# Head 0 of an attention kernel: half of K turned by the DMA engine, query halves shifted on chip, and head 1's K loaded later

## The chip, the cores and the metric

The kernel runs on one core of one Trainium2 chip. The metric is the device time of one execution in microseconds (us), as the median of several executions. The profile shows the work of TensorE (PE in the profile; PEld are its weight loads), VectorE (DVE), ScalarE (ACT), GpSimd (POOL) and SyncE (SP), side by side: in the kernel before PE is busy for 99% of the span, ACT for 60%, DVE for 33%, POOL for 15%. In its trace the DMA transfers are issued from the instruction streams of SP (K, V, x), POOL (W, the query moves) and ACT (the output, at 1751.7 to 1934.2 us), and engines wait for their landing, PE for instance 3.1 us for `xnT` (the list of waits below).

This case is about differences of 0.1 to 0.5%, so the scatter matters, and the document comes back to it.

## The reference, cut to what matters

```python
# B = 1, Sq = Sk = 2048, D = 640, H = 32 heads, Dh = 192, F = 1536; everything bf16
def _A_ref(x, k_cache, v_cache, wq, wo):
    q = (x @ wq) -> (B, H, Sq, Dh)
    scores = jnp.einsum("bhqd,bhkd->bhqk", q, k_cache) * (Dh ** -0.5)
    p = _softmax(scores, axis=-1)
    o = jnp.einsum("bhqk,bhkd->bhqd", p, v_cache)
    return o -> (B, Sq, H * Dh) @ wo

def _B_ref(x, w1, w3, w2):                      # SwiGLU feed-forward
    return (silu(x @ w1) * (x @ w3)) @ w2

x = A_x
xn = _layernorm(x, axis=-1)                     # no scale, no bias
return x + _A_ref(xn, ...) * silu(_B_ref(xn, ...))
```

## The kernel before: the parts that the change touches

The main loop walks over 32 heads, 4 query blocks of 512 rows (`qb`) and 8 steps (`p`), each step two key tiles. In every step PE makes the scores of step n + 2 and the values of step n. Once in every block it also projects the next head's queries for the same block. By the trace a step is 1.317 us of PE, a projection 2.16 us, and a steady block 12.69 us. What is special in head 0 is that everything has to be made ready first, while PE is already running:

- `xn`, the normalized x, is turned into `xnT` (D on the partitions). Blocks 0 and half of 1 are turned by PE, the rest by a transposing DMA.
- `xnS` is a copy of `xnT` with its two partition halves exchanged, made by two DMAs. The projections for head 1 and later need both.
- K is needed as five 128-wide windows of pairs of key rows (`KW`). Head 0's K is loaded plainly and turned by PE; later heads use a transposing DMA.
- `qC` holds shifted halves of the projected queries. Block 1 of head 0 shifts on DVE; the others by DMA from POOL (`move_q`).

`project0(qb)` projects head 0's own block qb; `project(1, qb)` projects head 1's block qb. The two are the landmarks of this document.

```python
    def load_k(h):


        pairs_of = A_k_cache[0, h].rearrange("(j two) d -> j (two d)", two=2)
        KW = kvp.tile([P, 5, HK], BF16, tag="KW", name="KW")
        nc.sync.dma_start_transpose(out=KW[:, 0:3, :], in_=pairs_of)
        nc.sync.dma_start_transpose(out=KW[:, 3:5, :], in_=pairs_of[:, 64:64 + 2 * P])
        loads.setdefault(h, {}).update(KW=KW)

    k0 = {}
    WINDOWS = (0, P, 2 * P, 64, 64 + P)

    def load_k0():
        k0["kn"] = stp.tile([P, NQT, HG * DH], BF16, tag="ostage", name="kn")
        kn = k0["kn"][:].rearrange("p t c -> p (t c)")[:, 0:NKT * DH]
        nc.sync.dma_start(out=kn, in_=A_k_cache[0, 0].rearrange("(p t) d -> p (t d)", p=P))
        k0["v"] = kn.rearrange("p (j c) -> p j c", c=2 * DH)
        loads.setdefault(0, {}).update(KW=kvp.tile([P, 5, HK], BF16, tag="KW", name="KW"))

    FIRST = (0, 1, 2, 4)

    def turn_k0(dst, j0, sel):
        for a in sel:
            w = WINDOWS[FIRST[a]]
            for b in range(NPAIR // 2):
                nc.tensor.transpose(out=dst[:, a, b * P:(b + 1) * P], in_=k0["v"][:, j0 + b, w:w + P],
                                    identity=ident_bf[:])

    def copy_k0(src, j0):
        KW = loads[0]["KW"]
        ks = slice(j0 * P, (j0 + NPAIR // 2) * P)
        nc.scalar.copy(out=KW[:, 0:2, ks], in_=src[:, 0:2, :])
        nc.scalar.copy(out=KW[:, 2:5:2, ks], in_=src[:, 2:4, :])

    def shift_k0(j0):
        KW = loads[0]["KW"]
        ks = slice(j0 * P, (j0 + NPAIR // 2) * P)
        nc.gpsimd.dma_start(out=KW[0:64, 3, ks], in_=KW[64:P, 0, ks])

    def load_v(h):
        vt = vts[h % 2]
        if h == 0:
            nc.sync.dma_start(out=vt[:, :, 0:DH], in_=A_v_cache[0, h].rearrange("(i s) d -> i s d", i=P))
        else:
            for t in range(2):
                nc.sync.dma_start(out=vt[:, :, 0:DH].rearrange("i (p t) d -> i p t d", t=2)[:, :, t, :],
                                  in_=A_v_cache[0, h].rearrange("(p i t) d -> i p t d", i=P, t=2)[:, :, t, :])
        loads.setdefault(h, {}).update(vt=vt)
# ... cut: the statistics and 1/sqrt(var + eps) of x: ln_stats, ln_stats_act, ln_rstd ...
    def ln_norm(g, i, engine):
        mv, _, rstd = lnorm[g]
        if (g, i) not in xns:
            xns[g, i] = xnp.tile([P, D], BF16, tag="xn", name="xn")
        engine.tensor_scalar(out=xns[g, i][:], in0=x_sb[:, 4 * g + i, :], scalar1=mv[:, i, 0:1], scalar2=rstd[:, i, 0:1],
                             op0=ALU.subtract, op1=ALU.mult)

    def ln_turn(g, i2, copy):
        pst = ps_st.tile([P, 2, DC, P], BF16, tag="st2", name="pst")
        for k in range(2):
            xn = xns.pop((g, 2 * i2 + k))
            for c in range(DC):
                nc.tensor.transpose(out=pst[:, k, c, :], in_=xn[:, c * P:(c + 1) * P], identity=ident_bf[:])
        q0 = (4 * g + 2 * i2) * P
        copy(out=xnT[:, :, q0:q0 + 2 * P].rearrange("p c (k q) -> p k c q", k=2), in_=pst[:])

    def ln_turn_dma(g, i):
        q0 = (4 * g + i) * P
        nc.sync.dma_start_transpose(out=xnT[:, :, q0:q0 + P], in_=xns.pop((g, i))[:])

    def swap_halves(g):
        qs = slice(g * 512, (g + 1) * 512)
        nc.sync.dma_start(out=xnS[0:64, :, qs], in_=xnT[64:P, :, qs])
        nc.sync.dma_start(out=xnS[64:P, :, qs], in_=xnT[0:64, :, qs])
# ... cut ...
    def move_q(qAB, qC, half):
        nc.gpsimd.dma_start(out=qC[0:64, half, :], in_=qAB[half][64:P, :])
        if half == 0:
            nc.gpsimd.dma_start(out=qC[64:P, 0, :], in_=qAB[0][0:64, :])
# ... cut ...
    def project0(qb):
        W = loads[0]["W"]
        qAB, qC = q_tiles(0, qb)
        qs = slice(qb * 512, (qb + 1) * 512)
        ps = ps_st.tile([P, 1024], F32, tag="st2", name="ps0")
        for half in range(2):
            for c in range(DC):
                nc.tensor.matmul(ps[:, half * 512:(half + 1) * 512], lhsT=W[:, half * DC + c, :], rhs=xnT[:, c, qs],
                                 start=(c == 0), stop=(c == DC - 1))
        cast_pair(qAB, ps)
        if qb == 1:
            nc.vector.tensor_copy(out=qC[64:P, 0, :], in_=qAB[0][0:64, :])
            nc.vector.tensor_copy(out=qC[0:64, 0, :], in_=qAB[0][64:P, :])
            nc.vector.tensor_copy(out=qC[0:64, 1, :], in_=qAB[1][64:P, :])
        else:
            move_q(qAB, qC, 0)
            move_q(qAB, qC, 1)
# ... cut ...
    def two_products(W, qs):

        ps = ps_st.tile([P, 1024], F32, tag="st2", name="ps")
        for j in range(2 * DC):
            for r in range(2):
                rows = slice(r * 64, (r + 1) * 64)
                xs = xnT if j % 2 == r else xnS
                nc.tensor.matmul(ps[:, r * 512:(r + 1) * 512], lhsT=W[rows, j, :], rhs=xs[rows, j // 2, qs],
                                 start=(j == 0), stop=(j == 2 * DC - 1))
        return ps

    def cast_pair(qAB, ps):
        a = nc.vector.tensor_copy(out=qAB[0][:], in_=ps[:, 0:512])
        b = nc.scalar.copy(out=qAB[1][:], in_=ps[:, 512:1024])

        tc.declare_no_dep(b.ins, a.ins, reason="two banks, two destinations")

    def project(h, qb):
        qAB, qC = q_tiles(h, qb)
        cast_pair(qAB, two_products(loads[h]["W"], slice(qb * 512, (qb + 1) * 512)))
        move_q(qAB, qC, 0)
        move_q(qAB, qC, 1)
# ... cut ...
        ov = [obanks[r][:].rearrange("p (j w) -> p j w", j=4)[:, :, 0:DH + 1] for r in range(2)]
        osum = osp.tile([P, 4, DH + 1], F32, tag="osum", name="osum")
        nc.vector.tensor_copy(out=osum[:], in_=ov[0])
        nc.vector.tensor_tensor(out=osum[:], in0=osum[:], in1=ov[1], op=ALU.add)
        osums[0] = osum
```

The start, the work hung onto the steps of head 0, and the loop:

```python
    def head_start():

        load_x(0, 0, 2)
        load_x(0, 2, 4)
        load_k0()
        load_w0()
        load_x(1)
        load_v(0)
        load_w(1)
        turn_over(40)
        ln_stats(0, 0)
        ln_stats(0, 1)
        ln_stats_act(0, 3)
        ln_stats(0, 2)
        ln_rstd(0, 3)
        ln_norm(0, 0, nc.vector)
        ln_norm(0, 1, nc.vector)
        ln_norm(0, 2, nc.vector)
        ln_norm(0, 3, nc.vector)
        pk0 = ps_o.tile([P, 4, 512], BF16, tag="ob0", name="pk0")
        turn_k0(pk0, 0, range(4))
        copy_k0(pk0, 0)
        shift_k0(0)
        turn_over(6)
        ln_turn(0, 0, nc.vector.tensor_copy)
        turn_over(6)
        turn_k0(pk1, NPAIR // 2, range(2))
        ln_turn(0, 1, nc.vector.tensor_copy)
        turn_k0(pk1, NPAIR // 2, range(2, 4))
        swap_halves(0)
        copy_k0(pk1, NPAIR // 2)
        shift_k0(NPAIR // 2)
        for g in range(2, NQB):
            load_x(g)
        project_first()
        scores(0)
        shift_first()
        scores(1)
        ln_stats(1, 0)
        ln_stats(1, 1)
        ln_stats(1, 2)
        ln_norm(1, 0, nc.vector)
        ln_norm(1, 1, nc.vector)
        ln_turn_dma(1, 0)
        ln_turn_dma(1, 1)
        ln_stats(1, 3)
# ... cut ...
    def first_head(qb, p):

        if qb == 0 and p == 1:
            ln_norm(1, 2, nc.vector)
            ln_norm(1, 3, nc.vector)
        if qb == 0 and p == 4:
            ln_turn(1, 1, nc.vector.tensor_copy)
            swap_halves(1)
        g = qb + 2
        if g < NQB:
            i = p - 2
            if 0 <= i < 4:
                ln_stats(g, i)
            for i2 in range(2):
                if p == (4, 6)[i2]:
                    for i in (2 * i2, 2 * i2 + 1):
                        ln_norm(g, i, nc.vector)
                        ln_turn_dma(g, i)
            if p == 6:
                swap_halves(g)
        if qb == 1 and p == 0:
            load_k(1)
            load_v(1)

    for n, (h, qb, p) in enumerate(stream):
        if p == 0 and n > 0:
            if h + 1 < H:
                project(h + 1, qb)
            else:
                ffn_open(qb)
        if h == 0 and qb == 0 and p == 3:
            project(1, 0)
        if h == 0 and qb + 1 < NQB and p == (5 if qb == 0 else 2):
            project0(qb + 1)
        scores(n + 2)
        values(n)
        if p == 0 and n > 0:
            finish_block(n - 1)
        if p == (5 if h == 0 else 2) and h < 2 * NPIG:
            swiglu(h, qb)
        if p == 4 and h + 1 == H:
            ffn_close(qb)
        if h == 0:
            first_head(qb, p)
```

`turn_over(k)` is a row of k dummy matmuls that keep PE going.

## Time and profile before

Before the change the kernel took 1953.1 us in the median of three executions, from 1952.4 to 1957.39. The execution that was profiled has a span of 1951.6 us.

| what | before | where it shows |
|---|---|---|
| PE busy | 1930.7 us, 99% of the span | the page, part 1 |
| PE's share of the chain that ended last | 97% | the page, part 4 |
| period of a block from head 1 on | 12.69 us | the PE timeline |
| first score matmul | 16.30 us | the PE timeline |
| `project(1, 3)` starts | 74.38 us | the PE timeline |

The first two lines are these, from the page of the kernel before (busy time, share and number of instructions of each engine; then the share of the chain that each engine holds):

```profile
...
PE 1930.7 (99%) x27281; PEld 1320.4 (68%) x27289; DVE 653.5 (33%) x991; ACT 1180.7 (60%) x1276; POOL 285.6 (15%) x510
...
PE 97%; DMA 1%; issue 0%; DVE 0%; POOL 0%; SPq 0%; DVEq 0%; POOLq 0%
...
```

PE is the bound. Only PE waits can be won, and after 74 us there are none. So the whole question lies in the first 75 us. I call the start of `project(1, 3)`, the first landmark after which the pattern repeats, **the mark**.

The waits of PE between 13 and 76 us, in the kernel before (what PE waited for, us in total, number of waits, the longest):

```profile
...
PE ps L407 <- DMA xnT<-xn: 3.1, 1, 3.1
PE st L489 <- DMA qC<-qA: 3.0, 1, 3.0
PE st L488 <- DMA KW<-KW: 1.0, 1, 1.0
PE ps L407 <- DVE xnT L354: 0.9, 1, 0.9
PE obank L517 <- DVE osum L527: 0.8, 1, 0.8
...
```

The view counts a wait from the modelled end of the last matmul, so it shows somewhat less than a stop costs in the distance between two landmarks. I use both.

The two largest waits come from the SP queue and the traffic behind it. The timeline of SP in the kernel before (start, duration, operation, destination and source):

```profile
...
38.23 2.52 SPq L358 DMA_TRANSPOSE xnT<-xn  x2
...
43.45 5.59 SPq L252 DMA_TRANSPOSE KW<-in_A_k_cache_dram  x1
49.08 4.28 SPq L253 DMA_TRANSPOSE KW<-in_A_k_cache_dram  x1
53.41 1.21 SPq L292 DMA_DIRECT2D vt<-in_A_v_cache_dram  x2
54.66 6.16 SPq L358 DMA_TRANSPOSE xnT<-xn  x4
...
```

An issue of a transposing load holds the SP queue for 4.28 and 5.59 us here. Head 1's K (L252, L253) and V stand in the queue ahead of the four transposes of xn (54.66), and the small `qC` moves of block 2 (64 KB each), issued at 45.98 to 46.99 us while K is moving, take 5.8 to 7.0 us to land, against a median of 1.9 us in this trace.

### The profile page before, as it was taken

To read this page: it belongs to the slowest core of one execution; us is meant where nothing else is said; L and a number is where in the kernel's file an instruction comes from. 1 tells how busy PE (TensorE), PEld (TensorE's weight loads), DVE (VectorE), ACT (ScalarE), POOL (GpSimd) and SP (SyncE) were. 2 spreads that over 40 slices of the span, in tenths; PEclk is the share of its full clock that TensorE was granted. 3 is DMA by queue.
4 is the path that set the end of the run, shared out by engine and by line. 5 is a ranking of instruction groups with operands and counts; after the bars stand their busy time and mean duration, and the time that the engine had idled before them with its cause. 6 is when DMAs were issued, how large, how long until landed. Compare 5 with 4: busy or idle time off the path is not lost.

```text
span 1951.6 us, 59687 instructions
## 1 busy us (share of the span) xinstructions
PE 1930.7 (99%) x27281; PEld 1320.4 (68%) x27289; DVE 653.5 (33%) x991; ACT 1180.7 (60%) x1276; POOL 285.6 (15%) x510
## 2 busy tenths in 40 slices
...
GB/s 179 135 66 92 52 98 63 90 66 97 63 97 68 100 68 100 68 157 67 100 68 100 68 99 65 100 68 79 87 61 90 59 81 2 239 81 138 154 152 60
DMA packets 394659, 179.50 MB, mean 92 GB/s; under 512 B 341632, under 2 KB 382848, under 8 KB 394400
## 3 DMA queue, kind: packets, MB, share of 16 engines
...
## 4 chain that ended last, share of the span: by engine, by line
PE 97%; DMA 1%; issue 0%; DVE 0%; POOL 0%; SPq 0%; DVEq 0%; POOLq 0%
PE obank L517 35%; PE st L488 33%; PE ps L425 14%; PE ps_s L111 11%; PE ps_f L723 3%; PE ps_gu L697 1%; PE st L489 1%; DMA x_all<-in_A_x_dram 0%; DMA kn<-in_A_k_cache_dram 0%; DMA qC<-qA 0%; PE ps L407 0%; DMA xnT<-xn 0%; DVE qA L430 0%; PE pk L272 0%; POOL rstd L325 0%
## 5 line engine op out<-in xcount | busy, mean ns | idle before, releaser
L491 ACT ACTIVATE pT<-st 128x1024 bf16<-128x1024 f32 x1024 | 1047.3, 1023 | 256.6 <-PE st L489 241.1
L517 PEld LDWEIGHTS <-pT 64*128 64x128 bf16 x16384 | 715.0, 94 | 242.5 <-issue 1.3
L517 PE MATMUL obank<-vt,pT 64*128 64x193 bf16 x16384 | 853.1, 243 | 0.8 <-DVE osum L527 0.8
L488 PE MATMUL st<-qC,KW 64*128 64x512 bf16 x2046 | 605.6, 376 | 1.2 <-DMA KW<-KW 1.0
L526 DVE COPY osum<-obank 128x772 f32<-128x772 f32 x128 | 123.2, 962 | 790.1 <-PE obank L517 790.1
L489 PE MATMUL st<-qC,KW 64*128 64x512 bf16 x1022 | 384.3, 376 | 3.0 <-DMA qC<-qA 3.0
L489 PE MATMUL st<-qB,KW 64*128 64x512 bf16 x1024 | 385.0, 376 | 0.0
L488 PE MATMUL st<-qA,KW 64*128 64x512 bf16 x1022 | 384.3, 376 | 0.3 <-ACT pT L491 0.3
L489 PE MATMUL st<-qA,KW 64*128 64x512 bf16 x1022 | 384.3, 376 | 0.0
L488 PEld LDWEIGHTS <-KW 64*128 64x128 bf16 x3068 | 277.9, 94 | 156.7 <-issue 5.5
L425 PE MATMUL ps<-xnT,W 64*128 64x512 bf16 x1280 | 297.3, 376 | 0.0
L425 PE MATMUL ps<-xnS,W 64*128 64x512 bf16 x1280 | 295.8, 376 | 0.0
L489 PEld LDWEIGHTS <-KW 64*128 64x128 bf16 x3068 | 278.1, 94 | 1.6 <-issue 0.5
L375 POOL DMA_DIRECT2D qC<-qA x126 | 66.2, 526 | 1293.6 <-DVE rl_all L533 1280.7
L431 ACT CAST qB<-ps 128x512 bf16<-128x512 f32 x131 | 76.8, 586 | 233.7 <-PE ps L425 223.3
L111 PE MATMUL ps_s<-wo_sb,oT 128*128 128x384 bf16 (+3 forms) x1535 | 208.8, 299 | 0.1
L425 PEld LDWEIGHTS <-W 64*128 64x128 bf16 x2560 | 123.4, 94 | 121.1 <-issue 0.2
L111 PEld LDWEIGHTS <-oT 128*128 128x128 bf16 x1536 | 148.3, 98 | 60.5
L527 DVE TENSOR_TENSOR osum<-osum,obank 128x772 f32<-128x772 f32 x128 | 122.7, 959 | 13.4
L534 DVE TENSOR_TENSOR ostage<-osum,rl_all 128x768 bf16<-128x768 f32 x128 | 122.6, 958 | 4.4
L466 DVE SCALAR_TENSOR_TENSOR hT<-pt,qB 64x512 bf16<-64x512 bf16 x64 | 43.8, 684 | 203.6 <-ACT pt L465 203.6
L430 DVE CAST qA<-ps 128x512 bf16<-128x512 f32 x131 | 90.6, 692 | 27.7 <-PE ps L407 9.8
...
## 6 DMA issues: line engine op xcount, KB each, us to landing
...
qC<-qA POOLq DMA_DIRECT2D x252, 64.0 KB, 1.9
...
```

The costliest lines, as they stand in the source:

```text
L111: nc.tensor.matmul(ps[:, 0:w], lhsT=oT[:, k, :], rhs=wo_sb[:, k, c0:c1], start=(k == 0), stop=(k == OC - 1))
L375: nc.gpsimd.dma_start(out=qC[0:64, half, :], in_=qAB[half][64:P, :])
L425: nc.tensor.matmul(ps[:, r * 512:(r + 1) * 512], lhsT=W[rows, j, :], rhs=xs[rows, j // 2, qs], start=(j == 0), stop=(j == 2 * DC - 1))
L430: a = nc.vector.tensor_copy(out=qAB[0][:], in_=ps[:, 0:512])
L431: b = nc.scalar.copy(out=qAB[1][:], in_=ps[:, 512:1024])
L488: nc.tensor.matmul(st2[:, 0:512], lhsT=ka, rhs=qa, start=r == 0 and nr == 3, stop=r == nr - 1)
L489: nc.tensor.matmul(st2[:, 512:1024], lhsT=kb, rhs=qb2, start=r == 0 and nr == 3, stop=r == nr - 1)
L491: nc.scalar.activation(out=pT2[:], in_=st2[:], func=ACT.Exp, scale=att_scale)
L517: nc.tensor.matmul(obanks[r][:, j * 256:j * 256 + DH + 1], lhsT=pT2[r * 64:(r + 1) * 64, t * 512 + j * P:t * 512 + (j + 1) * P], rhs=vt[r ...
L526: nc.vector.tensor_copy(out=osum[:], in_=ov[0])
L527: nc.vector.tensor_tensor(out=osum[:], in0=osum[:], in1=ov[1], op=ALU.add)
L534: nc.vector.tensor_tensor(out=ostage[:, qb * 4:qb * 4 + 4, hg * DH:(hg + 1) * DH], in0=osum[:, :, 0:DH], in1=rl.unsqueeze(2).to_broadcast( ...
```

## The change

The intent is to remove five losses of the start at once. Only the first half of head 0's K is turned by PE; the second half comes by a transposing load. K's shift and all query shifts of head 0 are made by DVE. The second turn of block 1 comes a step earlier, the second pair of norms of a later block comes behind the copies of the value banks (`osum`), and head 1's K and V are issued behind the last norms. The variance arithmetic is also regrouped (cut below; what it is worth was not measured).

```diff
@@ -254,43 +254,48 @@
         loads.setdefault(h, {}).update(KW=KW)
 
     k0 = {}
-    WINDOWS = (0, P, 2 * P, 64, 64 + P)
+    FIRST = (0, P, 2 * P, 64 + P)
+    HP = NPAIR // 2
 
     def load_k0():
-        k0["kn"] = stp.tile([P, NQT, HG * DH], BF16, tag="ostage", name="kn")
-        kn = k0["kn"][:].rearrange("p t c -> p (t c)")[:, 0:NKT * DH]
-        nc.sync.dma_start(out=kn, in_=A_k_cache[0, 0].rearrange("(p t) d -> p (t d)", p=P))
+        kn = stp.tile([P, NQT, HG * DH], BF16, tag="ostage", name="kn")
+        kn = kn[:].rearrange("p t c -> p (t c)")[:, 0:NPAIR * DH]
+        nc.sync.dma_start(out=kn, in_=A_k_cache[0, 0, 0:HK, :].rearrange("(p t) d -> p (t d)", p=P))
         k0["v"] = kn.rearrange("p (j c) -> p j c", c=2 * DH)
         loads.setdefault(0, {}).update(KW=kvp.tile([P, 5, HK], BF16, tag="KW", name="KW"))
 
-    FIRST = (0, 1, 2, 4)
-
-    def turn_k0(dst, j0, sel):
+    def load_k0_rest():
+        pairs_of = A_k_cache[0, 0, HK:SK, :].rearrange("(j two) d -> j (two d)", two=2)
+        KW = loads[0]["KW"]
+        nc.sync.dma_start_transpose(out=KW[:, 0:3, HP * P:HK], in_=pairs_of)
+        nc.sync.dma_start_transpose(out=KW[:, 3:5, HP * P:HK], in_=pairs_of[:, 64:64 + 2 * P])
+
+    def turn_k0(dst, sel):
         for a in sel:
-            w = WINDOWS[FIRST[a]]
-            for b in range(NPAIR // 2):
-                nc.tensor.transpose(out=dst[:, a, b * P:(b + 1) * P], in_=k0["v"][:, j0 + b, w:w + P],
+            for b in range(HP):
+                nc.tensor.transpose(out=dst[:, a, b * P:(b + 1) * P], in_=k0["v"][:, b, FIRST[a]:FIRST[a] + P],
                                     identity=ident_bf[:])
 
-    def copy_k0(src, j0):
+    def copy_k0(src):
         KW = loads[0]["KW"]
-        ks = slice(j0 * P, (j0 + NPAIR // 2) * P)
-        nc.scalar.copy(out=KW[:, 0:2, ks], in_=src[:, 0:2, :])
-        nc.scalar.copy(out=KW[:, 2:5:2, ks], in_=src[:, 2:4, :])
-
-    def shift_k0(j0):
+        nc.scalar.copy(out=KW[:, 0:2, 0:HP * P], in_=src[:, 0:2, :])
+        nc.scalar.copy(out=KW[:, 2:5:2, 0:HP * P], in_=src[:, 2:4, :])
+
+    def shift_k0():
         KW = loads[0]["KW"]
-        ks = slice(j0 * P, (j0 + NPAIR // 2) * P)
-        nc.gpsimd.dma_start(out=KW[0:64, 3, ks], in_=KW[64:P, 0, ks])
+        nc.vector.tensor_copy(out=KW[0:64, 3, 0:HP * P], in_=KW[64:P, 0, 0:HP * P])
 
     def load_v(h):
+
+
         vt = vts[h % 2]
+        p0 = 0
         if h == 0:
-            nc.sync.dma_start(out=vt[:, :, 0:DH], in_=A_v_cache[0, h].rearrange("(i s) d -> i s d", i=P))
-        else:
-            for t in range(2):
-                nc.sync.dma_start(out=vt[:, :, 0:DH].rearrange("i (p t) d -> i p t d", t=2)[:, :, t, :],
-                                  in_=A_v_cache[0, h].rearrange("(p i t) d -> i p t d", i=P, t=2)[:, :, t, :])
+            nc.sync.dma_start(out=vt[:, 0:NPAIR, 0:DH], in_=A_v_cache[0, h, 0:HK, :].rearrange("(i s) d -> i s d", i=P))
+            p0 = HP
+        for t in range(2):
+            nc.sync.dma_start(out=vt[:, 2 * p0:NKT, 0:DH].rearrange("i (p t) d -> i p t d", t=2)[:, :, t, :],
+                              in_=A_v_cache[0, h, 2 * p0 * P:SK, :].rearrange("(p i t) d -> i p t d", i=P, t=2)[:, :, t, :])
         loads.setdefault(h, {}).update(vt=vt)
 
     mhalf = const.tile([P, 4], F32, name="mhalf")
 # ... cut: the epsilon is added for two rows at once; ScalarE's statistics leave POOL out ...
@@ -388,8 +395,9 @@
                 for c in range(DC):
                     nc.tensor.matmul(ps[:, half * 512:half * 512 + 256], lhsT=W[:, half * DC + c, :], rhs=xnT[:, c, hs],
                                      start=(c == 0), stop=(c == DC - 1))
-            for half in range(2):
-                nc.vector.tensor_copy(out=qAB[half][:, hs], in_=ps[:, half * 512:half * 512 + 256])
+            i0 = nc.vector.tensor_copy(out=qAB[0][:, hs], in_=ps[:, 0:256])
+            i1 = nc.scalar.copy(out=qAB[1][:, hs], in_=ps[:, 512:768])
+            tc.declare_no_dep(i1.ins, i0.ins, reason="two banks, two destinations")
         nc.vector.tensor_copy(out=qC[0:64, 1, :], in_=qAB[1][64:P, :])
 
     def shift_first():
@@ -407,13 +415,9 @@
                 nc.tensor.matmul(ps[:, half * 512:(half + 1) * 512], lhsT=W[:, half * DC + c, :], rhs=xnT[:, c, qs],
                                  start=(c == 0), stop=(c == DC - 1))
         cast_pair(qAB, ps)
-        if qb == 1:
-            nc.vector.tensor_copy(out=qC[64:P, 0, :], in_=qAB[0][0:64, :])
-            nc.vector.tensor_copy(out=qC[0:64, 0, :], in_=qAB[0][64:P, :])
-            nc.vector.tensor_copy(out=qC[0:64, 1, :], in_=qAB[1][64:P, :])
-        else:
-            move_q(qAB, qC, 0)
-            move_q(qAB, qC, 1)
+        nc.vector.tensor_copy(out=qC[64:P, 0, :], in_=qAB[0][0:64, :])
+        nc.vector.tensor_copy(out=qC[0:64, 0, :], in_=qAB[0][64:P, :])
+        nc.vector.tensor_copy(out=qC[0:64, 1, :], in_=qAB[1][64:P, :])
 
     def two_products(W, qs):
 
@@ -575,36 +579,37 @@
         load_k0()
         load_w0()
         load_x(1)
+        load_k0_rest()
         load_v(0)
-        load_w(1)
         turn_over(40)
         ln_stats(0, 0)
         ln_stats(0, 1)
         ln_stats_act(0, 3)
         ln_stats(0, 2)
+        mv, ve, _ = lnorm[0]
+        nc.vector.tensor_scalar(out=ve[:, 2, :], in0=mv[:, 2, 1:2], scalar1=eps, scalar2=None, op0=ALU.add)
+        nc.vector.tensor_scalar(out=ve[:, 3, :], in0=lnorm["ss"][:], scalar1=1.0 / D, scalar2=eps,
+                                op0=ALU.mult, op1=ALU.add)
         ln_rstd(0, 3)
-        ln_norm(0, 0, nc.vector)
-        ln_norm(0, 1, nc.vector)
-        ln_norm(0, 2, nc.vector)
-        ln_norm(0, 3, nc.vector)
+        load_w(1)
+        for i in range(4):
+            ln_norm(0, i, nc.vector)
         pk0 = ps_o.tile([P, 4, 512], BF16, tag="ob0", name="pk0")
-        turn_k0(pk0, 0, range(4))
-        copy_k0(pk0, 0)
-        shift_k0(0)
-        turn_over(6)
-        ln_turn(0, 0, nc.vector.tensor_copy)
-        turn_over(6)
-        turn_k0(pk1, NPAIR // 2, range(2))
+        ln_turn(0, 0, nc.scalar.copy)
+        turn_over(4)
+        turn_k0(pk0, range(2))
+        turn_over(4)
         ln_turn(0, 1, nc.vector.tensor_copy)
-        turn_k0(pk1, NPAIR // 2, range(2, 4))
+        turn_k0(pk0, range(2, 4))
+        turn_over(4)
         swap_halves(0)
-        copy_k0(pk1, NPAIR // 2)
-        shift_k0(NPAIR // 2)
+        copy_k0(pk0)
         for g in range(2, NQB):
             load_x(g)
         project_first()
         scores(0)
         shift_first()
+        shift_k0()
         scores(1)
         ln_stats(1, 0)
         ln_stats(1, 1)
@@ -627,7 +632,7 @@
         if qb == 0 and p == 1:
             ln_norm(1, 2, nc.vector)
             ln_norm(1, 3, nc.vector)
-        if qb == 0 and p == 4:
+        if qb == 0 and p == 3:
             ln_turn(1, 1, nc.vector.tensor_copy)
             swap_halves(1)
         g = qb + 2
@@ -636,13 +641,13 @@
             if 0 <= i < 4:
                 ln_stats(g, i)
             for i2 in range(2):
-                if p == (4, 6)[i2]:
+                if p == (4, 7)[i2]:
                     for i in (2 * i2, 2 * i2 + 1):
                         ln_norm(g, i, nc.vector)
                         ln_turn_dma(g, i)
-            if p == 6:
+            if p == 7:
                 swap_halves(g)
-        if qb == 1 and p == 0:
+        if qb == 1 and p == 7:
             load_k(1)
             load_v(1)
 
@@ -654,7 +659,7 @@
                 ffn_open(qb)
         if h == 0 and qb == 0 and p == 3:
             project(1, 0)
-        if h == 0 and qb + 1 < NQB and p == (5 if qb == 0 else 2):
+        if h == 0 and qb + 1 < NQB and p == (5 if qb == 0 else 3):
             project0(qb + 1)
         scores(n + 2)
         values(n)
```

## The prediction

> **What bounds the kernel now.** TensorE: PE is 97% of the chain of waits, and from 74.5 us on the same line (head 1's projection for the last query block) recurs every 12.69 us without a gap. The change only touches the head, about 4% of the span; 2% (39 us) is out of reach. By the timeline, PE work between the first score (16.30 us) and 74.5 us is 26 score groups of 0.65, 24 value groups of 0.67, six projections of 2.16 and one turn of 0.56: 46.4 us in 58.2. About 12 us are lost there (PE timeline, waits):
> 1. 2 us before score group 2, for the K shift by DMA (KW<-KW, issued 12.3/14.9, landed 19.8/21.8).
> 2. 1.4 us at 28.6-30.3, projection waiting for xnT's copy after a late turn.
> 3. 1.1 us at 39.5, value group waiting for osum, behind two norms on DVE.
> 4. 3.1 us at 50.4-53.5, scores waiting for qC<-qA (7.0 us to land among head 1's K transposes; usually 1.9).
> 5. 3.1 us at 61.1-64.2, projection waiting for xnT<-xn, queued behind head 1's K (43.5-53.4) and V.
>
> **What the change does.** It halves the plain K load (768 to 384 KB) and adds a 512-row transposing load. PE loses 16 K transposes (0.06 us each), ACT two 1.0 us copies, but gains one xnT copy (estimate 1.2 us) and two half casts. DVE takes K's shift and the query shifts of blocks 2 and 3: 0.29 us each, in idle DVE time. Turn 1 moves to p=3, the second norms behind the osum copies, K1/V1 behind block 3's norms (about 57 us instead of 43; head 1 needs them at about 73, a whole K plus V took 15 us).
>
> **Costed.** Loss 4: -3.1. Loss 5: -2.6: the norms start about 2.1 us after the block's end, take 0.8, and the second transpose lands about 6.4 after it, where PE asks at 6.1; 0.3-0.6 us of wait stay, in block 1 too. Loss 3: -1.0. Loss 2: -1.2. Start and loss 1: PE alone could gain 4-5 us, but DMA is at 9 tenths nearly throughout 2-25 us, and bytes up to the xnS swap hardly fall (estimate 4.45 MB against 4.32). W0's last piece landed at 12.9, xnS at 23.0 (needed at 23.6), x block 2 at 25.0. If these stay, the first projection ends no earlier than 14.5 (now 15.5) and head 1's first begins no earlier than 22.5: gain about 1 us. [...]
>
> Sum: about 8 us. Predicted **1945.0 us, 1941.0 to 1949.5**. Faster by over 2%: 0.01; within 2%: 0.98; slower: 0.01.
>
> **What would show it.** The projection at 74.5 us starts at 66-67. No qC<-qA wait in head 0's scores; K1's transposes issued after 55 us; waits for xnT<-xn of at most 0.7 us each; first score near 15.0; project(1,0) at 22.5-23.5, after a wait for xnS; the 12.69 us period unchanged.
>
> **What would make it wrong.** A transposing load slow in the crowded start: K's second half, V and xnS come late and 1-3 us go. DMA lighter than I think: the gain is 11-12 us. Norms at p=7 pushing xnT later: 2-3 us return. K1 or V1 too late: head 1 stalls.

What is cut, at the end of "Costed", are two sentences of reasons for W0's slow landing and for the rate of the start that did not come from this case. No term of the sum is cut: losses 4, 5, 3 and 2 with 3.1, 2.6, 1.0 and 1.2 us and the start with about 1 make 8.9, less the 0.3 to 0.6 us of wait that stay in block 1; that is the "about 8". What the trace of before shows: W0's three loads on POOL (160, 80 and 80 KB) took 8.07, 8.70 and 9.38 us from issue to landing beside the loads on SP, and the core moved 334 GB/s from 7 to 10 us and 179 from 10 to 14. Why they were slow it doesn't show; that they would stay so was my estimate. The landing of `xnS` that the forecast gives as 23.0 us is 23.70 in that trace. The 1.2 us for a copy of `xnT` on ACT are an estimate; ACT's copy of K, four fifths as wide, took 1.02 us in before, and in after the copy of `xnT` took 1.23.

## The result, and the profile after

| | before | after |
|---|---|---|
| median of four fast runs (lowest to highest) | 1952.75 us (1948.89 to 1957.39) | 1950.75 us (1949.44 to 1952.48) |
| ratio, after over before | | 0.9989 (0.9965 to 1.0013) |
| span of the profiled run | 1951.6 us | 1947.9 us |
| the mark | 74.38 us | 70.77 us |

A ratio here stands on record with each timed set: it is worked out from the fast runs of both kernels in the same rounds, so it isn't quite the ratio of the medians. The brackets are a 95% interval. The class is "same" at 2%. The change gained about 2 us where 8 were predicted, and 1950.75 lies above the predicted range, 1941.0 to 1949.5.

The lines of the page of the kernel after that answer to those of before:

```profile
...
PE 1930.6 (99%) x27273; PEld 1318.3 (68%) x27273; DVE 653.1 (34%) x996; ACT 1179.5 (61%) x1277; POOL 282.5 (15%) x501
...
PE 97%; DMA 1%; DVE 1%; ACT 0%; issue 0%; POOL 0%; SPq 0%; POOLq 0%; DVEq 0%; ACTq 0%
...
```

PE does the same work in the same time; what changed is waiting. The waits of PE in the same window, in the kernel after:

```profile
...
PE ps L415 <- DMA xnT<-xn: 3.8, 2, 2.6
PE ps L429 <- DMA xnS<-xnT: 2.7, 1, 2.7
...
PE st L488 <- DVE qA L398: 0.6, 1, 0.6
...
```

The waits for `qC`, `osum` and `KW` are gone, as predicted. The wait for `xnT` is not smaller, it is larger: two waits, 3.8 us together, instead of one of 3.1. A wait for `xnS` of 2.7 us is new. 

The SP timeline shows where both come from. First the start, in the kernel before and then in the kernel after:

```profile
...
2.61 0.69 SPq L289 DMA_DIRECT2D vt<-in_A_v_cache_dram  x1
14.04 0.64 SPq L362 DMA_DIRECT2D xnS<-xnT  x1
14.72 0.62 SPq L363 DMA_DIRECT2D xnS<-xnT  x1
...
```

```profile
...
2.62 5.07 SPq L270 DMA_TRANSPOSE KW<-in_A_k_cache_dram  x1
7.74 3.63 SPq L271 DMA_TRANSPOSE KW<-in_A_k_cache_dram  x1
11.41 0.69 SPq L294 DMA_DIRECT2D vt<-in_A_v_cache_dram  x1
12.15 1.47 SPq L297 DMA_DIRECT2D vt<-in_A_v_cache_dram  x2
13.74 2.14 SPq L369 DMA_DIRECT2D xnS<-xnT  x1
15.92 0.62 SPq L370 DMA_DIRECT2D xnS<-xnT  x1
...
```

V's load was issued at 2.61 us before and is issued at 11.41 us after, because the two transposing loads hold the queue for 5.07 and 3.63 us. The swap into `xnS` is issued behind V, and lands at 24.2 us (23.7 before), although everything ahead of it was meant to be lighter. PE arrives at `project(1, 0)` at 21.21 us and stands there until 24.30.

Then blocks 1 and 2, in the kernel after:

```profile
...
38.94 2.52 SPq L365 DMA_TRANSPOSE xnT<-xn  x2
...
50.50 7.51 SPq L365 DMA_TRANSPOSE xnT<-xn  x4
61.81 0.60 SPq L369 DMA_DIRECT2D xnS<-xnT  x1
...
63.12 5.20 SPq L252 DMA_TRANSPOSE KW<-in_A_k_cache_dram  x1
```

Head 1's K (63.12) now stands behind everything, as intended. The transposes of block 1's second half are issued at 38.94 us, and those of block 2 at 55.48 (the last two of the four in the line of 50.50), but the landings are late, as the sums below show.

### Where the time went, stretch by stretch

A block of head 0 is 8 steps and two projections. By the trace's own durations that is 8 x 1.317 + 2 x 2.16 = 14.86 us of PE (an estimate from those). The distance from one `project(1, qb)` to the next, less 14.86, is what the block loses.

| stretch | before | after | gained | predicted |
|---|---|---|---|---|
| start of the span to `project(1, 1)` | 36.49 | 36.17 | 0.3 | about 2.2 (start 1, turn 1.2) |
| block 1: to `project(1, 2)` | 19.46 | 16.54 | 2.9 | 3.5 to 3.8 (4.1 less the rest wait) |
| block 2: to `project(1, 3)` | 18.43 | 18.06 | 0.4 | 2.6 |
| sum, the mark | 74.38 | 70.77 | 3.6 | about 8 |

So two terms failed: the start and block 2. Block 1 is some 0.7 us short, for the same reason as block 2, as will show.

The traces gain 3.6 us and the medians 2.0. The runs of the kernel before explain why the two need not agree. In the largest set (11 runs beside the third group of experiments) its times fall into two clusters, 1949.12 to 1949.73 (5 runs) and 1952.21 to 1953.76 (6 runs). The traced execution of before belongs to the upper cluster, that of after to the quick end of its own runs (1949.65). What puts an execution of before into one cluster or the other I have not traced.

### The profile page after: what moved, and what is told of

It reads as the page before. It is cut to its first block, busy times and chain, and to the rows that moved or that the text cites. A ratio compares the mean times of both kernels' runs of the same rounds, so it can differ in the third digit from the quotient of the medians.

```text
span 1947.9 us, 59661 instructions
## 1 busy us (share of the span) xinstructions
PE 1930.6 (99%) x27273; PEld 1318.3 (68%) x27273; DVE 653.1 (34%) x996; ACT 1179.5 (61%) x1277; POOL 282.5 (15%) x501
## 3 DMA queue, kind: packets, MB, share of 16 engines
q8 instruction: 215, 3.52, 0.8%
q10 hardware_dynamic: 2448, 2.62, 0.4%
## 4 chain that ended last, share of the span: by engine, by line
PE 97%; DMA 1%; DVE 1%; ACT 0%; issue 0%; POOL 0%; SPq 0%; POOLq 0%; DVEq 0%; ACTq 0%
PE obank L521 35%; PE st L492 33%; PE ps L429 14%; PE ps_s L111 11%; PE ps_f L728 3%; PE ps_gu L702 1%; PE st L493 1%; DMA W<-in_A_wq_dram 0%; DMA xnT<-xn 0%; DMA xnS<-xnT 0%; PE ps L415 0%; ACT pT L495 0%; PE ps L396 0%; DVE osum L530 0%; DVE stats L321 0%
## 5 line engine op out<-in xcount | busy, mean ns | idle before, releaser
L111 PE MATMUL ps_s<-wo_sb,oT 128*128 128x256 bf16 (+3 forms) x1536 | 208.8, 299 | 0.0
L111 PEld LDWEIGHTS <-oT 128*128 128x128 bf16 x1536 | 148.3, 98 | 60.5
L434 DVE CAST qA<-ps 128x512 bf16<-128x512 f32 x131 | 90.5, 691 | 28.9 <-PE ps L415 11.0
## 6 DMA issues: line engine op xcount, KB each, us to landing
o_scr<-ostage SPq DMA_DIRECT2D x16, 1536.0 KB, 10.2
```

The costliest lines, as they stand in the source:

```text
L111: nc.tensor.matmul(ps[:, 0:w], lhsT=oT[:, k, :], rhs=wo_sb[:, k, c0:c1], start=(k == 0), stop=(k == OC - 1))
```

## The experiments

### What each trace gave, in one table

All kernels gave correct results. "Time" is one single execution where n = 1; such a run has no state of its own, and I rest nothing on its time alone. The stretches come from each kernel's profiled execution.

| kernel | time (n) | before beside it | ratio (95%) | first score | to `project(1, 1)` | block 1 | block 2 |
|---|---|---|---|---|---|---|---|
| before | 1952.75 (4) | | | 16.30 | 36.49 | 19.46 | 18.43 |
| after | 1950.75 (4) | 1952.75 | 0.9989 (0.9965 to 1.0013) | 15.17 | 36.17 | 16.54 | 18.06 |
| b_k1late | 1951.58 (1) | 1950.63 | | 17.92 | 37.01 | 16.30 | 19.1 |
| b_shift | 1953.19 (1) | 1950.63 | | 17.97 | 37.10 | 16.30 | 20.97 |
| b_rest | 1945.09 (1) | 1950.63 | | 13.54 | 32.54 | 16.44 | 17.22 |
| a_p6 | 1948.44 (1) | 1950.63 | | 17.75 | 37.04 | 16.30 | 16.31 |
| a_movelate | 1952.47 (1) | 1952.30 | | 15.61 | 38.37 | 15.65 | 19.62 |
| a_pad | 1948.17 (1) | 1952.30 | | 15.32 | 36.30 | 16.54 | 16.58 |
| a_early | 1945.84 (1) | 1952.30 | | 15.43 | 36.49 | 15.44 | 15.06 |
| a_reorder | 1947.32 (1) | 1952.30 | | 14.46 | 33.97 | 16.38 | 18.13 |
| after_again | 1950.54 (5) | 1952.21 | 0.9997 (0.9984 to 1.0010) | 16.74 | 36.68 | 16.52 | 18.00 |
| b_rest_again | 1948.38 (5) | 1952.21 | 0.9985 (0.9972 to 0.9998) | 14.26 | 33.63 | 16.48 | 17.44 |
| best1 | 1943.68 (5) | 1952.21 | 0.9962 (0.9949 to 0.9975) | 14.88 | 33.36 | 15.60 | 15.06 |
| best2 | 1946.57 (6) | 1952.21 | 0.9973 (0.9960 to 0.9987) | 17.57 | 36.25 | 16.33 | 15.06 |
| a_w0act | 1947.40 (1) | 1952.16 | | 16.42 | 34.32 | 16.45 | 17.92 |
| a_kplain | 1946.63 (5) | 1952.16 | 0.9972 (0.9959 to 0.9986) | 15.52 | 33.65 | 16.59 | 17.16 |
| best3 | 1945.00 (5) | 1952.16 | 0.9960 (0.9946 to 0.9974) | 16.24 | 34.92 | 17.25 | 15.06 |
| best4 | 1944.10 (5) | 1952.16 | 0.9958 (0.9944 to 0.9971) | 15.58 | 34.05 | 16.02 | 15.06 |
| after_third | 1951.64 (5) | 1954.04 | 0.9988 (0.9974 to 1.0002) | 17.78 | 43.26 | 16.55 | 17.75 |
| best6 | 1943.22 (5) | 1954.04 | 0.9949 (0.9936 to 0.9963) | 15.52 | 33.65 | 15.49 | 15.06 |

Read the column "first score" first. The kernels b_k1late, b_shift and b_rest have exactly the start code of before, up to that matmul. Theirs is at 17.92, 17.97, 13.54 and 14.26 (b_rest_again), before's at 16.30. The same instructions, up to 4.4 us apart. Two causes show. The first load of K landed at 9.8 us in before and at 7.1 in b_rest. And where it landed alike, in before and in b_k1late, the clock differed. These are the first matmuls after it, in the PE timeline of before and then of b_k1late (start, duration, and in brackets the wait ahead):

```profile
...
9.85 1.07 PE L272 MATMUL pk<-ident_bf,kn 128*128 128x128 bf16 x16 [2.65 <-DMA kn<-in_A_k_cache_dram]
...
```

```profile
...
9.85 1.32 PE L272 MATMUL pk<-ident_bf,kn 128*128 128x128 bf16 x16 [2.65 <-DMA kn<-in_A_k_cache_dram]
...
```

The wait is the same 2.65 us, but in b_k1late the granted clock is 0.50 from 11 to 13 us and in before it stays 1.00; the first score is 1.6 us later. So a single execution cannot tell whether a start is 1 us better, and the first score alone is no evidence; the distance from the first score onward, and timed rounds, are.

### Theory and rivals

My theory after the first result: (S) in the start, the transposing load holds the SP queue and moves slowly in the crowd, so that V and the swap come late; (N) the second norms, put behind `osum`, make xnT late, and they do so in both blocks. The rivals: (R1) K's load of head 1 was never the cause of loss 5, so moving it gained nothing; (R2) the traffic of the query moves, which now meets the transposes, makes xnT late; (R3) the new start is good and what is lost is lost in blocks 1 and 2 only.

### First group: one part alone on the kernel before, and one part undone on the kernel after

**b_k1late** is the kernel before with head 1's K and V issued at step 6 of block 1 instead of step 0.

```diff
@@ -644,3 +644,3 @@
                 swap_halves(g)
-        if qb == 1 and p == 0:
+        if qb == 1 and p == 6:
             load_k(1)
```

> The kernel before, with one part of the change alone: head 1's K and V are issued behind the last norms' transposes (block 1, p=6) instead of at its p=0. Mark: start of head 1's projection for the last query block, 74.5 us before, 70.9 after. Theory A (head 1's K in the DMA queue made both waits): the qC<-qA wait of 3.1 us and the xnT<-xn wait of 3.1 us both fall below 1 us, mark 68.3 to 69.5. Rival B (the wait for xnT<-xn has another cause, as it is still there in the changed kernel: the q moves and an instruction fetch landing in the same microseconds): the qC wait falls to below 0.5, the xnT wait stays above 1.5, mark 70 to 71.5.

**b_shift** is the kernel before with all query shifts of head 0 on DVE.

```diff
@@ -409,3 +409,3 @@
         cast_pair(qAB, ps)
-        if qb == 1:
+        if qb > 0:
             nc.vector.tensor_copy(out=qC[64:P, 0, :], in_=qAB[0][0:64, :])
```

> The kernel before, with the query shifts of blocks 2 and 3 on DVE alone; head 1's K stays early. Theory A: the qC<-qA wait of 3.1 us goes, the xnT<-xn wait of 3.1 us stays or grows a little (the transposes are still queued behind K), mark 71 to 72.5. Rival: taking the wait away only moves PE forward into the same late xnT (K1 sets its landing, at 64.0), so that the xnT wait doubles to 5 to 6 us and the mark stays at 74 to 74.6.

**b_rest** is everything of the change but the new start: the DVE shifts, the turn at step 3, the norms and the swap at step 7, head 1's K at step 7 and `project0` at step 3, on the kernel before.

```diff
@@ -410 +410 @@
-        if qb == 1:
+        if qb > 0:
@@ -630 +630 @@
-        if qb == 0 and p == 4:
+        if qb == 0 and p == 3:
@@ -639 +639 @@
-                if p == (4, 6)[i2]:
+                if p == (4, 7)[i2]:
@@ -643 +643 @@
-            if p == 6:
+            if p == 7:
@@ -645 +645 @@
-        if qb == 1 and p == 0:
+        if qb == 1 and p == 7:
@@ -657 +657 @@
-        if h == 0 and qb + 1 < NQB and p == (5 if qb == 0 else 2):
+        if h == 0 and qb + 1 < NQB and p == (5 if qb == 0 else 3):
```

> All of the change except its start: head 0's K is still loaded whole and turned by TensorE and shifted by DMA; query shifts on DVE, turn 1 at p=3, norms and swap at p=7, project0 at p=3, K1 late. If the new start was worth the predicted 1 us or more, the mark is at 72 or later (after: 70.9). If the start was worth nothing, since the DMA queue holds xnS and x back in either start, the mark is at 70.3 to 71.3, with project(1,0) at about 23.6 without a wait.

**a_p6** is the kernel after with the second norms and the swap back at step 6.

```diff
@@ -644 +644 @@
-                if p == (4, 7)[i2]:
+                if p == (4, 6)[i2]:
@@ -648 +648 @@
-            if p == 7:
+            if p == 6:
```

> The changed kernel with the second pair of norms and the swap back at p=6. Theory A (the norms behind the osum copies are what makes xnT late): xnT<-xn lands 1.5 to 2.5 us earlier against the block's end, the waits of 1.3 and 3.1 us of project0(2) and (3) fall to under 0.5 each, a wait for osum of about 1 us returns in front of the first value group of block 1 and perhaps 2; mark 68 to 69.5. Rival B (the q moves and the instruction fetch): the transposes come before the q moves, so they also land sooner, but the osum wait eats it: mark 70 to 71.

Measured. The waits of PE from 13 to 76 us, first of b_shift, then of b_k1late:

```profile
...
PE ps L407 <- DMA xnT<-xn: 3.2, 1, 3.2
PE obank L517 <- DVE osum L527: 1.6, 2, 0.8
...
```

```profile
...
PE st L489 <- DMA qC<-qA: 2.6, 1, 2.6
PE obank L517 <- DVE osum L527: 1.6, 2, 0.8
...
```

In b_shift the `qC` wait is gone and block 1 falls from 19.46 to 16.30 us. But block 2 grows from 18.43 to 20.97: PE now comes to `project0(3)` three microseconds earlier, and xnT, still behind head 1's K in the queue, lands only 1.4 us earlier (about 62.7 us; its swap was issued at 64.10 in before and at 62.72 here). The wait has only moved on. In b_k1late the `xnT` wait and block 1's `qC` wait are both gone, but K's transposing loads, issued at 60.35 us, now meet the query moves of block 3: a `qC` wait of 2.6 us turns up at 69.96. So losses 4 and 5 stand in series and have one cause, the K load in the middle of head 0. Either repair alone leaves most of the loss in place; with both (b_rest) no `qC` wait is left, and the waits for xnT, 1.0 and 1.8 us, are those of the late norms (below). R1 falls: K's load was the cause of loss 5 in the kernel before.

By the mark (72.40, 74.37, 66.20 and 69.65 us in b_k1late, b_shift, b_rest and a_p6) my expectations did badly: of the ranges that I had written down, only that of b_shift's rival was hit, and b_rest came earlier than both of its own. The mark carries the scatter of the start with it, so from here I go by the stretches and the waits.

There is a third cost in b_shift. The same ten matmuls of `project0(3)`, in the PE timeline of the kernel after and then of b_shift (start, duration, and in brackets the idle time ahead of it):

```profile
...
61.92 2.32 PE L415 MATMUL ps<-xnT,W 128*128 128x512 bf16 x10 [2.65 <-DMA xnT<-xn]
...
```

```profile
...
62.84 3.69 PE L407 MATMUL ps<-xnT,W 128*128 128x512 bf16 x10 [3.24 <-DMA xnT<-xn]
...
```

and the window 63 to 64 us of b_shift (busy time of each engine, then the granted clock, the DMA share and GB/s):

```profile
...
63.00:64.00 1.00, 1.00 (x3) 0.30 (x2) 0.00 (x0) 0.00 (x0) 0.00 (x0) 0.50 0.08 20
...
```

The granted clock was 0.50 there. After a wait of 3.24 us PE ran at half speed for a while, and the 2.32 us took 3.69.

b_rest was 5.5 us ahead of the before run beside it (1945.09 against 1950.63), and its first score came early by luck, so it was timed again later.

a_p6 shows what the late norms do. The waits of PE in a_p6:

```profile
...
PE obank L521 <- DVE osum L531: 1.6, 2, 0.8
PE ps L429 <- DMA xnS<-xnT: 1.0, 1, 1.0
...
```

No wait for xnT is left; the `osum` wait is back, 0.8 us in each block. Block 1 is 16.30 instead of 16.54, block 2 is 16.31 instead of 18.06. The step of the change that was meant to save 1 us, the norms behind `osum`, costs 0.2 us net in block 1 and 1.75 in block 2 (of which a_pad, below, puts 1.5 down to something else). N holds.

### Second group: why do xnT's transposes land late, and does the order in the start matter?

In the kernel after, block 1: the norms start at 38.47 us, 2.3 after the block's end (36.17; I had said 2.1), the transposes are issued at 38.94, and the last lands at about 43.7, 7.6 us after the block's end. In block 2 they start at 55.02, again 2.3 after the end (52.71), and land at about 61.65, 8.9 after it. I had said 6.4. So the norms start when I said, and the transposes fly too long. What delays them, and why more in block 2?

**a_movelate** delays the query moves of `project(1, 1)` and `project(1, 2)` to step 6, which takes them from under the transposes. It tests R2.

```diff
@@ -438,2 +438,4 @@
 
+    late = []
+
     def project(h, qb):
@@ -441,2 +443,5 @@
         cast_pair(qAB, two_products(loads[h]["W"], slice(qb * 512, (qb + 1) * 512)))
+        if h == 1 and qb in (1, 2):
+            late.append((qAB, qC))
+            return
         move_q(qAB, qC, 0)
@@ -663,2 +668,6 @@
             project0(qb + 1)
+        if late and p == 6:
+            qAB, qC = late.pop()
+            move_q(qAB, qC, 0)
+            move_q(qAB, qC, 1)
         scores(n + 2)
```

> The changed kernel; head 1's q moves of blocks 1 and 2 (three DMAs of 64 KB each from POOL) are issued at p=6 instead of right after the projection, so that they no longer share the DMA engines with xnT's second transposes. Measured from the start of head 1's projection in block 1 to its start in block 3, since the loads at the kernel's start vary from run to run (this stretch: before 38.05 us, changed 34.76, norms at p=6 32.61, PE work alone 29.7). Contention theory: xnT lands about 0.9 us sooner in block 1 (2.6 us after issue instead of 3.5) and about 1 sooner in block 2, stretch 32.8 to 33.6. Rival (the moves cost nothing, only the late norms and an instruction fetch do): stretch 34.4 to 35.0.

**a_pad** puts 44 dummy matmuls of 128x128 (88 instructions on PE with their weight loads) ahead of `project(1, 0)`. It is meant to shift the instruction fetches against the program. The profile shows them as DMA packets on a queue of their own: q8 "instruction" on the page of the kernel after, 215 packets and 3.52 MB, so 16 KB each. One is seen at 57.8 us in the kernel after.

```diff
@@ -421,5 +421,7 @@
 
-    def two_products(W, qs):
+    def two_products(W, qs, pad=0):
 
         ps = ps_st.tile([P, 1024], F32, tag="st2", name="ps")
+        for i in range(pad):
+            nc.tensor.matmul(ps[:, 0:P], lhsT=ident_bf[:], rhs=ident_bf[:], start=True, stop=True)
         for j in range(2 * DC):
@@ -440,3 +442,3 @@
         qAB, qC = q_tiles(h, qb)
-        cast_pair(qAB, two_products(loads[h]["W"], slice(qb * 512, (qb + 1) * 512)))
+        cast_pair(qAB, two_products(loads[h]["W"], slice(qb * 512, (qb + 1) * 512), 44 if (h, qb) == (1, 0) else 0))
         move_q(qAB, qC, 0)
```

> The changed kernel with 44 dummy 128x128 matmuls (88 PE instructions) in front of project(1,0), inside its wait for xnS: no other instruction moves, but the 16 KB instruction fetch seen at 57-58 us, amid block 2's xnT transposes, should come about 3 us earlier, before they start. Fetch theory: block 2's xnT<-xn lands 3.5 us after issue instead of 4.9, its wait falls from 3.1 to about 1.6 us, block 1's stays 1.5; stretch 33.0 to 33.6. Rival: the long landing has nothing to do with the fetch; block 2's wait stays at 2.7 to 3.2, stretch 34.4 to 35.0.

**a_early** moves the norms early enough that neither DVE's `osum` nor PE's projection has to wait: the statistics of block 3 two steps earlier, the norms at steps 4 and 6 (for block 2) and 3 and 4 (for block 3), and one gate product off DVE's way.

```diff
@@ -640 +640 @@
-            i = p - 2
+            i = p - 2 + 2 * qb
@@ -644 +644 @@
-                if p == (4, 7)[i2]:
+                if p == ((4, 6), (3, 4))[qb][i2]:
@@ -648 +648 @@
-            if p == 7:
+            if p == (6, 4)[qb]:
@@ -668 +668 @@
-        if p == (5 if h == 0 else 2) and h < 2 * NPIG:
+        if p == (7 if (h, qb) == (0, 0) else 5 if h == 0 else 2) and h < 2 * NPIG:
```

> The changed kernel with the norms early enough that DVE waits for nothing: block 1 takes the statistics of x's last group at p=0 to 3 and normalizes at p=3 and 4; block 0 at p=4 and 6 with its swiglu step moved behind the osum copies. If the place of the norms in DVE's queue is all that held back the xnT gain, both xnT<-xn waits fall under 0.3 us, no osum wait over 0.4 returns, stretch 29.8 to 30.8. If the transposes are slow for another reason, waits of over 1 us remain and the stretch is 32 or more.

**a_reorder** moves the swap of xnS and the load of x block 3 behind the transposes of block 1, and `project(1, 0)` from step 3 to step 7.

```diff
@@ -604,6 +604,4 @@
         turn_over(4)
-        swap_halves(0)
         copy_k0(pk0)
-        for g in range(2, NQB):
-            load_x(g)
+        load_x(2)
         project_first()
@@ -620,2 +618,4 @@
         ln_turn_dma(1, 1)
+        swap_halves(0)
+        load_x(3)
         ln_stats(1, 3)
@@ -659,3 +659,3 @@
                 ffn_open(qb)
-        if h == 0 and qb == 0 and p == 3:
+        if h == 0 and qb == 0 and p == 7:
             project(1, 0)
```

> The changed kernel with the start's DMA queue in order of need: x's third group and the transposes of xnT's second group go in front of block 0's half swap and x's fourth group, and project(1,0), which nothing in head 0 needs, moves from p=3 to p=7. From the first score to head 1's projection in block 1 (PE work alone 16.7 us; before 20.2, 19.1, 19.1, changed 21.0, 19.3): if the start is bound by the DMA queue's bytes in front of x and xnS, 16.8 to 18.3 us, with no wait for xnS; if the waits only move to x or xnT, 19 to 21 us. The xnT waits of blocks 1 and 2 stay as in the changed kernel.

Measured, a_movelate: in block 1 the distance from `project(1, 1)` to `project0(2)` falls from 7.70 to 6.81 us (PE's own work there is 6.11), so the moves cost xnT 0.9 us in block 1. In block 2 the experiment failed: block 1's delayed moves were issued only at 55.2 to 56.3 us, just ahead of block 2's transposes, and block 2's at 58.0 to 59.0, among them, so they were not really late; a wait of 2.5 us stayed and was followed by half clock (the ten matmuls took 4.01 us). R2 is right for block 1, and this run says nothing on block 2.

Measured, a_pad: the DMA view shows the packet. First the window of 57 to 58 us in the kernel after, then the same window in a_pad (the queues with their packets, megabytes and share of the window of 16 engines; then issues, with the us from issue to landing):

```profile
...
q8 instruction: 1, 0.02, 9.9%
...
xnT<-xn SPq DMA_TRANSPOSE x1, 4.9
```

```profile
...
q1 hardware_dynamic: 534, 0.13, 67.1%
...
xnT<-xn SPq DMA_TRANSPOSE x1, 3.5
```

One instruction packet of 16 KB took 9.9% of 16 us, which is 1.58 us of one DMA engine. Twenty 256-byte packets of the transpose that began while it ran, from 58.80 to 59.02 us, took 1.3 to 1.5 us each in the packet records, where their median is 0.018 (that they are those of the fetch's engine is inferred; the records kept here do not name the engine). They end at 60.3 to 60.4 us, the last packets of the transpose at 60.5, and it lands at 61.68: 4.9 us from issue to landing. In a_pad the fetch falls at 54 to 55 us, and the transposes land in 3.5 us, as they do in block 1 of the kernel after. Block 2 falls from 18.06 to 16.58 us, while block 1 stays at 16.54 to the digit. (The dummies themselves cost nothing: they ran while PE would have waited for `xnS`.) In the kernels whose instruction stream up to there is as in after, block 2 took 18.06, 18.00, 17.75, 18.13 and 17.92 us (after, after_again, after_third, a_reorder, a_w0act), so it isn't one unlucky execution. The whole difference between blocks 1 and 2 of the kernel after, 1.5 us, is therefore put down to an instruction fetch that happened to fall under the last transpose. Nothing in the change intends that; it is where the instruction stream stood.

Measured, a_early: block 1 is 15.44, block 2 is 15.06, no `xnT` or `osum` wait is left. The waits of PE:

```profile
...
PE ps L429 <- DMA xnS<-xnT: 2.7, 1, 2.7
PE ps L396 <- DMA W<-in_A_wq_dram: 1.8, 1, 1.8
...
PE st L492 <- DVE qA L434: 0.2, 1, 0.2
```

So 4.1 us lie in the placing of the norms (and of the gate product that moved with them): 1.1 in block 1, 3.0 in block 2. This is more than an undoing: a_p6, which only puts the norms back, has 16.30 and 16.31. Of block 2's, 1.5 are the fetch, and a transposition that starts earlier has the room to absorb it. The times agree as far as single runs can: 1945.84 against 1952.3 of before beside it.

Measured, a_reorder: the `xnS` wait is gone, but a wait of 1.44 us for V comes at 18.78 us, since V is still behind the transposing loads. From the first score to `project(1, 1)` it took 19.5 us; in the kernel after 21.0. I had expected 16.8 to 18.3: a miss, the gain was about half of what I thought.

### Third group: timed comparisons

Five rounds each, on one chip: the kernel after as it is (**after_again**), b_rest as it is (**b_rest_again**), **best1**, which is the kernel after with the edits of a_reorder and a_early together, and **best2**, which is b_rest with the same repairs (so it differs from best1 by the start).

```diff
 # best1 = a_reorder + a_early on the kernel after; best2: the same edits on b_rest
-            i = p - 2
+            i = p - 2 + 2 * qb
-                if p == (4, 7)[i2]:
+                if p == ((4, 6), (3, 4))[qb][i2]:
-            if p == 7:
+            if p == (6, 4)[qb]:
-        if h == 0 and qb == 0 and p == 3:
+        if h == 0 and qb == 0 and p == 7:
 # and swap_halves(0), load_x(3) behind ln_turn_dma(1, 1)
```

> The changed kernel once more, timed in five rounds beside the kernel before, and with a second profile of its start. My theory: the rest of the head gains 3 to 4 us in every run, the new start gains nothing on average and scatters by 2 us with the loads; ratio to the kernel before 0.9975 to 0.999. Rival (the single traces mislead and the change is worth the predicted 8 us, or nothing): 0.996 or 1.000.

> All of the change but its new start (K whole, turned by TensorE, shifted by DMA). Its one trace so far had the first score at 13.5 us, where three other kernels with the same start had 16.3 to 18.0. If that was luck with the loads: first score at 16 to 18 in this profile and a ratio like after_again's within 0.001. If the new start with its transposing load costs time (the queue was held 8.7 us by it and V issued at 11.4 instead of 2.6): b_rest_again faster than after_again by 0.001 to 0.002.

> The changed kernel with both repairs: the DMA queue of the start in order of need with project(1,0) at p=7 (a_reorder), and the norms of blocks 0 and 1 early enough (a_early). If the two gains add: the stretch from head 1's projection in block 1 to block 3 is 30 to 31 us, that projection starts in block 1 at 33.5 to 35.5, in block 3 at 64 to 66 (changed 70.9), ratio 0.994 to 0.996. If they collide in the DMA queue: stretch over 32.

> Both repairs on the old start (K whole, turned by TensorE, shifted by DMA). If the transposing load costs the start time, this is faster than best1 by 0.5 to 2 us; if the new start is worth its on-chip shift and shorter K load, best1 is faster by as much.

Measured: after_again 0.9997 (0.9984 to 1.0010), so the change as it stands is not shown to be faster than before at all in these rounds, and my own range (0.9975 to 0.999) was missed. b_rest_again 0.9985 (0.9972 to 0.9998), which leaves the new start out. The intervals overlap, but four of its five runs (1945.9 to 1948.97; the fifth is 1950.21) lie under the lowest of after_again (1950.06). So the new start gained nothing, and probably lost about 2 us. R3 falls. best1 is 0.9962 and best2 0.9973: with the same repairs in both, the new start is no longer behind. best1's stretch from `project(1, 1)` to block 3 is 30.66 us, so the two gains add as expected; the ratio is just outside the 0.994 to 0.996 that I had stated.

### Fourth group: what is slow in the start

Between 8 and 12 us the core's DMA moves little in the kernel after. The windows view (window and length; busy time of PE, PEld, DVE, ACT and POOL with instructions; granted clock; packet time as a share of the 16 engines, over 1 where packets overlap; GB/s), before and then after:

```profile
...
8.00:12.00 4.00, 2.15 (x39) 2.15 (x40) 1.42 (x5) 1.04 (x2) 0.69 (x1) 1.00 1.07 251
...
```

```profile
...
8.00:12.00 4.00, 3.62 (x53) 3.30 (x51) 1.79 (x4) 2.34 (x3) 2.51 (x4) 1.00 1.29 128
...
```

The engines' packet time is full in both (1.07 and 1.29), but in the kernel after they move half as much: 128 GB/s instead of 251. This is no single unlucky trace: the eight others with the transposing load and W0 on POOL have 91 to 137 GB/s in the same window (137 in after_again), the five others with the old start 195 to 232. Two candidates work in that window: the transposing load of K from SP and the small packets of W0, head 0's projection weights, from POOL. Take away each.

**a_kplain** loads K's second half plainly too (3 KB more per partition), turns it on PE into the free bank, copies it by DVE, shifts both halves by DVE, and brings V in two plain halves. Everything else is the kernel after.

```diff
     def load_k0_rest():
-        nc.sync.dma_start_transpose(out=KW[:, 0:3, HP * P:HK], in_=pairs_of)
-        nc.sync.dma_start_transpose(out=KW[:, 3:5, HP * P:HK], in_=pairs_of[:, 64:64 + 2 * P])
+        nc.sync.dma_start(out=k0["kn"][:, NPAIR * DH:NKT * DH],
+                          in_=A_k_cache[0, 0].rearrange("(p t) d -> p (t d)", p=P)[:, NPAIR * DH:NKT * DH])
     # ... cut: V's layout follows; shift_k0 shifts both halves ...
+        turn_k0(pk1, range(4), HP)
         swap_halves(0)
-        copy_k0(pk0)
+        copy_k0(pk0, nc.scalar.copy)
+        copy_k0(pk1, nc.vector.tensor_copy, HP)
```

> The changed kernel with one part undone: the second half of head 0's K is loaded plainly behind x's second group (393 KB in rows of 3 KB) and turned by TensorE, with DVE doing its two copies and the shift; the transposing load (two issues, 655 KB written) is gone. Theory A (the transposing load moves little per microsecond, 150 GB/s in 7.7-11.4 us against 282 before, and holds V, xnS and x back): xnS lands at 21.5 to 23 instead of 24.2 to 25.1, project0(1) starts 1.5 to 3 us earlier than the 30.0 to 30.8 of the changed kernel, ratio 0.9975 to 0.9988 (after_again 0.9997). Rival B (it is the bytes and the queue's order, not the transposes): xnS at 24 or later, ratio within 0.0006 of after_again's.

**a_w0act** issues W0's three loads from ACT instead of POOL.

```diff
@@ -223,3 +223,3 @@
-        nc.gpsimd.dma_start(out=W[:, 0:DC, :], in_=A_wq[:, 0:P].rearrange("(c p) d -> p c d", p=P))
-        nc.gpsimd.dma_start(out=W[:, DC:2 * DC, 0:PGW], in_=gate_cols(0).rearrange("(c p) f -> p c f", p=P))
-        nc.gpsimd.dma_start(out=W[:, DC:2 * DC, PGW:P], in_=A_wq[:, P:DH].rearrange("(c p) d -> p c d", p=P))
+        nc.scalar.dma_start(out=W[:, 0:DC, :], in_=A_wq[:, 0:P].rearrange("(c p) d -> p c d", p=P))
+        nc.scalar.dma_start(out=W[:, DC:2 * DC, 0:PGW], in_=gate_cols(0).rearrange("(c p) f -> p c f", p=P))
+        nc.scalar.dma_start(out=W[:, DC:2 * DC, PGW:P], in_=A_wq[:, P:DH].rearrange("(c p) d -> p c d", p=P))
```

> The changed kernel with W0's three loads issued from ACT's queue instead of POOL's. If W0's landing (12.6 to 13.9 us) is what sets the first score, it lands before 10, the first score comes at 13.0 to 14.0 instead of 15.2 to 17.8. If the start is bound by the bytes in front of xnS and not by the first score, project(1,0) still stands waiting for xnS until 24 to 25 and project0(1) starts at 29.5 to 31 as before: nothing gained. Rival: the gain of the first score is kept, project0(1) at 28 to 28.7.

**best3** is best1 with a_kplain, **best4** is best1 with a_w0act.

> best1 (ratio 0.9962) with K's second half loaded plainly and turned by TensorE. If the transposing load costs time even with the queue in order of need: V's first half lands 1 to 2 us sooner and the ratio is 0.9950 to 0.9958. If best1's order hides it: 0.9958 to 0.9966.

> best1 with W0 issued from ACT's queue. With the xnS wait out of the way the first score should count: first score at 13 to 14 instead of 14.9, V's first half (17.7 to 18.7 us) becomes the next wait, so that about half of it stays: ratio 0.9955 to 0.9962.

Measured. The same window in a_kplain and in a_w0act:

```profile
...
8.00:12.00 4.00, 3.16 (x54) 2.91 (x53) 1.91 (x4) 2.59 (x3) 2.64 (x4) 1.00 1.11 268
...
```

```profile
...
8.00:12.00 4.00, 3.70 (x35) 3.70 (x36) 1.54 (x4) 1.23 (x1) 3.07 (x4) 1.00 1.35 238
...
```

Both are back at 268 and 238 GB/s. In a_kplain the swap is issued at 11.10 and 11.85 us and lands at 20.9 (24.2 after); the `xnS` wait is gone; `project(1, 1)` comes at 33.65 us instead of 36.17, with the first score later than in the kernel after (15.52 against 15.17), so the 2.5 us are won behind it. Timed: 0.9972 (0.9959 to 0.9986). In a_w0act the transposing loads are kept, and land at 10.8 and 12.6 us instead of 13.3 and 16.5, the swap lands at 22.4, and no `xnS` wait shows; `project(1, 1)` comes at 34.32. Its expectation missed all the same: I had expected the first score at 13 to 14 us, and it came at 16.42. PE no longer waited for W0 there. But DVE could begin with x only at 4.29 us (3.76 in the kernel after), the row of dummy matmuls ended 2.48 us before the first turn, and PE then turned at half pace: eight transposes of K took 1.06 us, against 0.61. The trace's first clock record, full speed, comes at 13.52 us in a_w0act and at 8.75 in the kernel after; the views write 1.00 for the time before it, which is not measured.

So taking away either one ends the slow spell: with the transposing load out of the way, or with W0 issued from ACT, the window has 238 GB/s or more (best3, best4 and best6 repeat it: 269, 248 and 275). What it is about W0 is less clear than it looks. The edit of a_w0act changes the queue and the time: W0's packets on ACT's queue are through by 9 us but for 42, and from 10 to 11 us the transposing load has the engines to itself, at 287 GB/s. While they overlapped, from 8 to 9 us, the core moved 187. And in after_again the low rate outlasts W0: 85 GB/s from 12 to 13 us, with one POOL-issued packet. So that the packets come from POOL is not shown to matter; what both edits removed is most of the time in which W0 and the transposing load move together. In the kernel after a packet of the hardware queue takes about 61 ns in this window (1100 packets hold 104.7% of 64 engine-us, an estimate from the DMA view); in a_w0act about 23 ns (2609 packets hold 94.5%). Which of the two slows the other, and how, the runs don't tell.

best3 and best4 are 0.9960 and 0.9958, not told apart from best1's 0.9962 of the round before: on top of best1's order the cure of the start gives nothing visible. (best4's first score missed its range of 13 to 14 us too: 15.58.) best1 had already taken the swap out of the way, and in best3's trace the swap, issued late, now makes PE wait 1.8 us in block 1.

### Fifth group: the two faults undone together

**after_third** is the kernel after once more; **best6** is the kernel after with a_kplain and a_early and nothing else, so with the start's transposing load and the late norms undone, and the rest of the change kept. (a_early puts the norms earlier than they were before the change, so this is a little more than an undoing.)

```diff
 # best6 = a_kplain + a_early, as shown above; after_third: no edit
```

> The changed kernel again, on the same chip and in the same rounds as best6: ratio to the kernel before 0.9985 to 1.0 as in its other two timings; first score between 15 and 18 us, xnS landed between 24 and 25.2, waits for xnT of about 1.1 and 2.6 us in blocks 1 and 2.

> The changed kernel with its two faults undone and nothing else: K's second half loaded plainly (a_kplain, ratio 0.9972) and the norms early (a_early, stretch 30.5 us). If the two account for the missing gain and add: head 1's projection starts in block 1 at 33 to 34.5, the stretch from there to block 3 is 30 to 31 us, so block 3 at 63.5 to 65 (changed kernel 70.9), ratio 0.9950 to 0.9962. If they collide (xnT's transposes earlier, beside other loads): ratio 0.9965 or more.

Measured: best6 1943.22 us (1943.05 to 1944.28) against 1954.04, a ratio of 0.9949 (0.9936 to 0.9963). Its waits of PE from 13 to 76 us are only these:

```profile
...
PE st L491 <- DVE qA L401: 0.6, 1, 0.6
PE st L495 <- ACT pT L498: 0.3, 1, 0.3
PE st L495 <- DVE qA L437: 0.2, 1, 0.2
```

The mark is at 64.20 us, 10.2 earlier than before's; the medians differ by 10.8. after_third, on the same chip and in the same rounds, was 0.9988 (0.9974 to 1.0002): the two intervals do not overlap. after_third's profiled run was its slowest (1956.31) and shows how far the crowded start can go: PE waited 0.7 us for V at 21.4, the swap landed at 28.9 us after a wait of 3.9, outside the 24 to 25.2 that I had expected, and the clock was halved from 27 to 33 us; `project(1, 1)` came at 43.26.

## Why the prediction was wrong, point by point

**Right.** PE is the bound and only head 0 was touched; the period stayed 12.69 us. Loss 4 (`qC`) is gone, loss 3 (`osum`) is gone, K's shift is off the path, head 1's K was issued at 63.1 us (after 55, as said) without stalling head 1. The first score came at 15.17 ("near 15.0"), but the same start code gave 15.32 to 17.78 in six other traces (a_pad, a_early, a_movelate, after_again, a_p6, after_third), so that hit is partly luck. 2% was out of reach.

**Wrong, first step: "the second transpose lands about 6.4 after it ... 0.3-0.6 us of wait stay, in block 1 too."** It landed 7.6 and 8.9 us after the block's end, and the waits were 1.1 and 2.65 us in the view; in distance between the landmarks (7.70 and 9.21 us where PE's work is 6.11) 1.6 and 3.1. The norms began when I said they would (2.3 after, said 2.1). What failed was the flight time of the transposes: in block 2 it was 4.9 us from issue with the fetch, and 3.5 without (a_pad). Counted from the start of the norms to the issue of the swap, which waits for the last transpose, it took 4.4 us in the kernel before (37.76 to 42.13); 2.1 and 4.4 come close to the predicted 6.4, so the prediction seems to have carried that time over (an inference, it does not say). In the kernel after it took 5.4 us in block 1 and 6.8 in block 2; without the query moves 4.4 again (a_movelate, block 1), without the fetch 5.3 (a_pad, block 2). The causes are shown: the query moves beside them cost 0.9 us in block 1 (a_movelate), and an instruction fetch 1.5 us in block 2 (a_pad). a_early, where both still happen but early enough, recovers 4.1 us. Loss 5 was rightly put on head 1's K for the kernel before (b_k1late), but it wasn't removed: the change took one cause away and put another in its place. I had listed it, "Norms at p=7 pushing xnT later: 2-3 us return", and gave it too little weight.

**Wrong, second step: "bytes up to the xnS swap hardly fall ... gain about 1 us".** I counted bytes at the rate of before. In the kernel after the rate in 8 to 12 us is half (128 GB/s against 251), the two transposing loads hold the SP queue from 2.62 to 11.4 us, and so V is issued at 11.41 instead of 2.61. Landing of xnS got worse, 24.2 instead of the 23.0 that I counted with, and `project(1, 0)` stood until 24.30 (said: 22.5 to 23.5). By the first score to `project(1, 1)` stretch the new start (21.0 in after, 19.9 and 19.3 in after_again and a_p6, 21.1 and 22.8 in a_early and a_movelate, 25.5 in after_third) isn't better than the old one (20.2 in before, 19.1 in b_shift and b_k1late, 19.0 and 19.4 in b_rest and b_rest_again), although the late turn of before, loss 2, lies in this stretch and is gone in the new one. a_kplain, with the transposing load taken out, has 18.1. This risk too was listed: "A transposing load slow in the crowded start ... 1-3 us go." I had not counted with a rate that halves where W0 meets the transposing load.

**The sum.** 8.4 us were predicted by stretches: 2.2 in the start, 3.6 in block 1, 2.6 in block 2. The traces gave 0.3, 2.9 and 0.4. The start's missing 1.9 and the 2.9 missing in blocks 1 and 2 are the two faults; best6, which repairs just those two, gains 10.2 us at the mark. By stretches that is 2.8, 4.0 and 3.4: 0.4 to 0.8 us more than I had predicted in each. Part of that is a_early's own, which also leaves no `osum` wait. With a_p6's blocks (16.30 and 16.31) behind best6's start (33.65) the mark would be at 66.26, a gain of 8.1 us; this is an estimate, such a kernel was not run. So with the two faults gone the costing of the losses was about right.

**The scatter.** The yardstick itself moves. The prediction was set against 1953.1, the median of three runs; with later runs before lies between 1948.89 and 1957.39. The three timed sets of the unchanged kernel after give 0.9989, 0.9997 and 0.9988, so the change is worth between 0.6 and 2.3 us by these, and none of the three intervals excludes zero.

One source of it shows, as in the pair of lines under the table: after some PE waits the granted clock is 0.50 for a while, in some executions only. I saw it, by the clock in the views, in eight of the twenty traces (b_k1late, b_shift, a_p6, a_movelate, after_again, after_third, best2, best4), after waits of 2.2 to 3.9 us. Summed from views of one us each it was 0.50 for about 3.4 us in b_k1late, b_shift, best2 and best4 at the start; in after_third it was halved from 27 to 33 us. The same wait for `xnS` was followed by it in a_movelate (2.70 us; from 26 us on two matmuls of the projection take 0.67 us) but not in after and a_early (2.71 and 2.72 us; two matmuls keep taking 0.40 us, and the clock of after is 1.00 from 24 to 27 us). Why only some executions are hit the traces don't show.

**What stays open.** What the late transposes of block 2 owe to the query moves (a_movelate failed there; the 0.9 us that stay in a_pad, 5.3 less 4.4, would fit, but no run shows it). Which of the two slows the other in the crowded start (transposing load, W0), and whether W0's queue or only its time matters. Why a PE wait of 2.7 us is followed by a clock of 0.50 in one execution and not in another. Why the same start code lands K at 7.1 us in one execution and 9.8 in another. What, beside such halvings, separates the two clusters of the kernel before.
